# A linear-attention layer and MLP on one core: the issue order of the attention phase redone

## The chip, the cores and the metric

The kernel runs on one core of a Trainium2 chip. The metric is the device time of one execution in microseconds (us); the median of several executions is given. Five engines work at the same time, each through its own list of instructions in order: TensorE (PE, matmuls; PEld is its weight load), VectorE (DVE), ScalarE (ACT), GpSimd (POOL) and SyncE (SP, whose queue issues most of the DMAs here). An engine that reaches an instruction whose inputs are not ready stops there, and everything behind it in its list stops too. All runs quoted are fast, that is, none was slowed as a whole.

## The reference, cut to what matters

```python
h   = x + A(layernorm(x))        # S = 2048 tokens, D = 576, 32 heads of 18
out = h + B(layernorm(h))
def A(y):                        # linear attention
    q, k, v = heads(y @ wqkv)
    phi(t) = [softmax(t @ w_phi), softmax(-t @ w_phi)]
    kv, z = sum over tokens of phi(k) * v, and of phi(k)
    return (phi(q) @ kv / (phi(q) @ z)) @ wo
def B(y):                        # MLP, F = 4608
    return gelu(layernorm(y) @ w1 + b1) @ w2 + b2
```

The tokens are cut into 16 tiles of 128. Phase 1 must see every tile's k and v before any attention output exists, since kv is a sum over all tokens. After it come attention output, wo and MLP, in 8 rounds of two tiles.

## The kernel before

A small scheduler records every operation with what it reads and writes, in *program order*, and derives the waits from that: a read recorded after a write waits for that write. So moving a line changes the order in which an engine meets its work, and sometimes also what it waits for. `yT` holds normalised, transposed tiles in NSL slots; tile t uses slot t % NSL.

```python
NSL = 10
# start, SP queue: the wk transposes first, then a transpose for each normalised tile
# phase 1 (cut):
for t in range(NT + 2):
    if t < NT: p1_k(t)                     # k of tile t, two exponentials on ScalarE
    if t in (3, 4): ...weffq_unit(i)...    # folds w_phi into wq; needs the wq transposes
    if 5 <= t < NT: fill(1)                # one q unit: q of two tiles, 7 or 14 heads
    if t == 0:
        ln1_norm("pool", 4); ln1_tr(4)     # normalise on GpSimd, transpose by DMA on SP
        ln1_norm("pool", 5); ln1_tr(5)
        for b, (h0, nh) in enumerate(HG):
            dma_tr(wqT[...])               # five wq transposes, behind tiles 4 and 5
    ... p1_v(t - 1); p1_kv(t - 2); p1_mul(t - 1); p1_sums(t) ...
    for u in {0: (6,), 1: (7,), 2: (8,), 3: (9,), 7: (10,), 8: (11,), 10: (12,), ...}.get(t, ()):
        ln1_norm("pool", u); ln1_tr(u)
    for _ in range(2): bulk.pop(0)()       # two bulk weight loads a tile
# after it (cut): N = phi(q) @ kv, then wo, LN2, and the MLP
for r in range(NR):
    if r == 0:                             # the first three W1 groups split by tile
        for j in range(2):
            for g in range(3): w1_group(0, g, 128 * j, 128)
    for g in range(NG):                    # NG = 9
        if r or g >= 3: w1_group(r, g)
        if more and g == (0 if r else 3): attn_N(a, S1)
        if more and g == (4 if r else 6):
            attn_wo(a, S1)
            attn_N(b, S1)                  # same PSUM banks as wo
    slots[12] = lambda b=b: attn_wo(b, S1) # inside the first W2 tile, 41 steps
    w2_tile(r, 0, slots); w2_tile(r, 1, {})
```

The softmax here doesn't subtract the row's maximum and nothing guards it: scores larger than these inputs give would overflow.

## Time and profile before

| reading | value | from |
|---|---|---|
| time | 474.74 us | median |
| TensorE busy | 424.4 us of 475.4 | page |
| start of k(0), of k(5) | 17.2, 52.1 us | timeline |
| start of the MLP | 129.7 us | timeline |
| MLP round 0, a later round | 54.3, 41.64 us | timeline, chain |

The head of the page of the kernel before: busy tenths of TensorE in 40 slices of 11.9 us each, and the clock it was granted.

```profile
span 475.4 us, 8941 instructions
PE   2456996987888999999999999999999999999996
...
PEclk9995898998979799999999999999999999999999
```

The last two thirds are full; TensorE's idle time is in the first third, so that is where order can gain most. Lines of TensorE picked from the view of waits of the kernel before (who waited for whom: us in total, times, longest):

```profile
PE ps_all L415 <- DMA RA<-in_A_wqkv_dram: 6.8, 5, 2.2
PE ps_all L496 <- DVE RA L423: 6.3, 1, 6.3
PE ps_all L496 <- DMA yT<-ybuf: 5.0, 3, 2.3
PEld ps_all L596 <- DVE x_all L643: 5.5, 7, 0.8
PE ps_all L596 <- DVE x_all L643: 4.3, 7, 0.6
```

In order: the wq transposes, the folded wk before k(0), tiles normalised too late, and, seven times, N waiting for VectorE to drain the banks of wo. The timeline of TensorE at k(5) and around the late tiles (start us, us, engine, line, operation, shapes, count; in brackets the idle time just before and who ended it):

```profile
52.06 1.58 PE L496 MATMUL ps_all<-RA,yT 128*128 128x512 bf16 x10
...
74.06 1.39 PE L496 MATMUL ps_all<-RA,yT 128*128 128x512 bf16 x10 [1.69 <-DMA yT<-ybuf]
...
77.05 0.72 PE L546 MATMUL ps_all<-RB 128*128 128x133 bf16 x10
80.09 2.56 PE L496 MATMUL ps_all<-RA,yT 128*128 128x512 bf16 x10 [2.32 <-DMA yT<-ybuf]
```

The same block of k takes 1.39 us after the wait of 1.69 us and 2.56 after that of 2.32: matmuls after idle time can be slow for a while.

### The profile page before, as it was taken

The numbers are of one execution on the slowest core, as the hardware profiler recorded it, in microseconds if no ns is written. First come the engines' busy times: TensorE is split into PE (matmuls) and PEld (weight loads), VectorE is DVE, ScalarE is ACT, GpSimd is POOL, SyncE is SP. The second block draws the span as 40 slices with busy tenths as digits, with TensorE's granted clock in tenths as the row PEclk, the third lists the DMA queues.
The fourth block names the chain that finished last, engine by engine and source line by source line (L and its number), as shares of the span: only waits on it lengthen the run. The fifth ranks groups of instructions, "written<-read, shape, count | busy, mean of one in ns | idle before, by whom it ended". The sixth has DMA issues, their size and how long they took to land.

```text
span 475.4 us, 8941 instructions
## 1 busy us (share of the span) xinstructions
PE 424.4 (89%) x3702; PEld 271.5 (57%) x3702; DVE 190.6 (40%) x456; ACT 186.9 (39%) x422; POOL 78.8 (17%) x105
## 2 busy tenths in 40 slices
PE   2456996987888999999999999999999999999996
PEld 1123663655666546655765666576566657656753
DVE  3663596778502433331443333144333314431002
ACT  3343582533777302530650254066025406602710
POOL 2992348200001100110110011011001101100000
PEclk9995898998979799999999999999999999999999
DMA  8568956100251010102110011112001111100000
GB/s 189 134 128 247 278 176 181 39 2 14 48 195 17 14 34 21 25 18 28 28 30 17 23 23 21 28 28 27 17 26 22 22 28 28 28 15 26 2 0 26
DMA packets 51952, 26.76 MB, mean 56 GB/s; under 512 B 39752, under 2 KB 50888, under 8 KB 51912
## 3 DMA queue, kind: packets, MB, share of 16 engines
q1 hardware_dynamic: 50736, 25.58, 22.0%
q10 hardware_dynamic: 1176, 0.61, 0.7%
q8 instruction: 29, 0.48, 0.4%
q14 instruction: 11, 0.09, 0.1%
HBM read 14.47 MB, written 2.36 MB: 35 GB/s over the span
## 4 chain that ended last, share of the span: by engine, by line
PE 75%; DVE 7%; POOL 5%; DMA 5%; ACT 3%; issue 2%; SPq 1%; ACTq 1%; DVEq 0%; POOLq 0%
PE ps_all L798 29%; PE ps_all L775 26%; PE ps_all L769 5%; PE ps_all L637 4%; POOL ybuf L367 3%; PE ps_all L496 3%; PE ps_all L511 3%; PE ps_all L576 2%; DMA oT<-obuf 2%; PE ps_all L596 2%; DMA yT<-ybuf 2%; SPq L321 1%; DMA x_all<-in_A_x_dram 1%; PE ps_all L546 1%; DVE x_all L643 1%
## 5 line engine op out<-in xcount | busy, mean ns | idle before, releaser
L780 ACT ACTIVATE RA<-ps_all,b1T 128x256 bf16<-128x256 f32 (+1 forms) x300 | 125.8, 462 | 196.2 <-PE ps_all L775 192.2
L775 PE MATMUL ps_all<-yT,w1sb 128*128 128x256 bf16 (+1 forms) x1200 | 142.6, 274 | 0.0
L775 PEld LDWEIGHTS ps_all<-yT,w1sb 128*128 128x128 bf16 x1200 | 110.5, 100 | 27.2 <-issue 15.1
L798 PE MATMUL ps_all<-w2a,RA 128*128 128x512 bf16 (+1 forms) x640 | 95.3, 286 | 0.0
L798 PE MATMUL ps_all<-RB,RA 128*128 128x64 bf16 (+1 forms) x512 | 67.7, 286 | 0.0
L798 PEld LDWEIGHTS ps_all<-w2a,RA 128*128 128x128 bf16 x640 | 46.5, 98 | 36.2
L798 PEld LDWEIGHTS ps_all<-RB,RA 128*128 128x128 bf16 x512 | 33.4, 98 | 32.3
L643 DVE SCALAR_TENSOR_TENSOR x_all<-ps_all,x_all 128x576 bf16<-128x576 f32 x16 | 12.1, 757 | 94.4 <-PE ps_all L637 94.4
L628 POOL TENSOR_TENSOR obuf<-tpn 128x576 bf16<-128x576 f32 x14 | 19.6, 1401 | 165.5 <-issue 138.6
L804 DVE TENSOR_TENSOR tmpo<-ps_all,b2bc 128x64 f32<-128x64 f32 x16 | 3.6, 225 | 100.6 <-PE ps_all L798 100.6
L496 PE MATMUL ps_all<-RA,yT 128*128 128x512 bf16 (+1 forms) x160 | 27.0, 323 | 12.7 <-DVE RA L423 6.3
L502 ACT ACTIVATE RB<-ps_all 128x576 bf16<-128x576 f32 x32 | 19.1, 648 | 39.5 <-PE ps_all L496 39.5
L532 DVE TENSOR_TENSOR RB<-ps_all,RB 128x1152 bf16<-128x1152 f32 x16 | 21.6, 1350 | 29.6 <-PE ps_all L511 29.5
L656 POOL TENSOR_TENSOR st<-st,neghalf 128x1 f32<-128x1 f32 x16 | 8.8, 548 | 141.6 <-DVE st L654 141.6
L367 POOL TENSOR_SCALAR ybuf<-x_all,st 128x576 bf16<-128x576 bf16 x14 | 32.1, 2299 | 0.7 <-POOL st L347 0.4
L769 PE MATMUL ps_all<-yT,w1t 64*128 64x256 bf16 (+1 forms) x300 | 29.9, 274 | 2.3 <-ACT RA L780 2.3
L582 ACT ACTIVATE Eq<-ps_all 128x512 bf16<-128x512 f32 (+1 forms) x48 | 25.3, 527 | 16.0 <-DVE den L612 9.9
L576 PE MATMUL ps_all<-yT,WQ 128*128 128x256 bf16 x200 | 26.6, 285 | 1.9 <-ACT Eq L582 1.9
L511 PE MATMUL ps_all<-RB,yT 128*128 128x512 bf16 (+1 forms) x160 | 25.3, 310 | 1.3 <-DVE RB L532 1.3
L637 PE MATMUL ps_all<-wo_sb,oT 128*128 128x512 bf16 (+1 forms) x160 | 23.0, 292 | 3.3 <-DMA oT<-obuf 3.3
L496 PEld LDWEIGHTS ps_all<-RA,yT 128*128 128x128 bf16 x160 | 11.9, 108 | 24.2 <-issue 16.6
L576 PEld LDWEIGHTS ps_all<-yT,WQ 128*128 128x128 bf16 x200 | 19.4, 103 | 7.1 <-ACT Eq L582 2.7
(76 smaller groups left out, 290.3 us busy)
## 6 DMA issues: line engine op xcount, KB each, us to landing
w1sb<-in_B_w_dram SPq DMA_DIRECT2D x8, 576.0 KB, 5.1
w2a<-in_B_w_dram SPq DMA_DIRECT2D x4, 720.0 KB, 7.9
RB<-in_B_w_dram SPq DMA_DIRECT2D x2, 1152.0 KB, 7.5
out_dram<-WQ SPq DMA_DIRECT2D x16, 144.0 KB, 1.7
x_all<-in_A_x_dram SPq DMA_DIRECT2D x3, 576.0 KB, 4.4
RB<-in_A_wqkv_dram SPq DMA_DIRECT2D x1, 576.0 KB, 5.7
w1t<-in_B_w_dram SPq DMA_DIRECT2D x2, 288.0 KB, 8.0
wo_sb<-in_A_wo_dram SPq DMA_DIRECT2D x1, 576.0 KB, 9.2
```

Source lines behind the costliest of these rows:

```text
L367: P.add(eng, lambda e: e.tensor_scalar(ybuf[yb][:, 0:D], src, mean, rstd, ALU.subtract, ALU.mult), reads=[r_src, r_st], writes=[res(f"ybuf ...
L496: P.add("pe", lambda e, c=c, o=o, n=n: e.matmul(ps_all[:, 512 * KB + o:512 * KB + o + n], yT[:, c, sl * 128:(sl + 1) * 128], weffk[:, c, o ...
L511: P.add("pe", lambda e, c=c, o=o, n=n: e.matmul(ps_all[:, 512 * VB + o:512 * VB + o + n], yT[:, c, sl * 128:(sl + 1) * 128], wv[:, c, o:o ...
L532: P.add("dve", lambda e: e.tensor_tensor(vx(t)[:, :, :, 0:DH], ps_all[:, 512 * VB:512 * VB + D].rearrange("p (h d) -> p h d", h=H).unsquee ...
L576: P.add("pe", lambda e, i=i, c=c, h0=h0: e.matmul(ps_all[:, 512 * bk + RW * i:512 * bk + RW * i + RW], weffq[:, c, DH * h0:DH * h0 + 128], ...
L582: P.add("act", lambda e, s=s: e.activation(Eq[:, r, s, bs[0]:bs[0] + n, :], ps_all[:, 512 * bk:512 * bk + RW * n].rearrange("p (b t) -> p ...
L628: P.add(oeng, lambda e: e.tensor_tensor(obuf[ob][:, 0:D], tpn[:, 0, :], tpn[:, 1, :], ALU.add), reads=[res("tpn")], writes=[res(f"obuf{ob}")])
L637: P.add("pe", lambda e, c=c, bk=bk, o=o, n=n: e.matmul(ps_all[:, 512 * bk:512 * bk + n], oT[ob][:, c, :], wo_sb[:, c, o:o + n], start=(c = ...
L769: P.add("pe", lambda e, i=i, o=o, h=h, w=w: e.matmul(ps_all[:, o:o + n], w1t[h:h + 64, w:w + 128], yT[h:h + 64, 4, ys], start=(i % 2 == 0) ...
L775: P.add("pe", lambda e, c=c, m=m, o=o: e.matmul(ps_all[:, o:o + n], w1sb[:, c, 128 * m:128 * m + 128], yT[:, c, ys], start=False, stop=(c ...
L780: P.add("act", lambda e, m=m, o=o: e.activation(hmid[:, m, off:off + n], ps_all[:, o:o + n], AF.Gelu_apprx_tanh, bias=b1T[:, m:m + 1]), re ...
L798: P.add("pe", lambda e, m=m, bk=bk, o=o, n=n: e.matmul(ps_all[:, 512 * bk:512 * bk + n], w2_lhs(m, j), w2_rhs(m, o, n), start=(m == 0), st ...
```

## The change

The intent was to keep TensorE fed before the MLP, and to take two small waits out of each round. Its core:

```diff
-    NSL = 10
+    NSL = 12
+    def warm(n):                      # dummy matmuls on a zeroed tile
+        for _ in range(n):
+            P.add("pe", lambda e: e.matmul(ps_all[:, 2048:2560], WQ[:, 0:128], WQ[:, 128:640], ...
+    warm(12)                          # before the first real matmul, and 2 or 3 after each weffk group
...                                    # wq transposes interleaved with those of tiles 1 to 3
-    for t in range(NT + 2):
+    WU = {2: (0, 1), 3: (2, 3), 4: (4, 5, 6)}
+    for t in range(NT):
+        for u in ((4, 5) if t == 1 else (t + 4,) if 1 < t < NT - 4 else ()):
+            ln1_norm("pool", u)       # four tiles ahead, before the work of tile t
+            ln1_tr(u)
+        p1_k(t)
+        for i in WU.get(t, ())[:1]:
+            weffq_unit(i)
+        if t >= 5:
+            fill(1)
...                                    # the bulk loads: one or two a tile, from tile 1 on
-        P.add("dve", ... tmpo = psum + b2 (two pieces); ostage = tmpo + x)   # condensed
+        P.add("pool", ... tmpo = x + b2)                                     # condensed
+        P.add("dve", ... ostage = psum + tmpo, in two pieces)                # condensed
...
-        if r == 0: (three W1 groups split by tile)
-            if more and g == (4 if r else 6):
+            if more and g == 5:
                 attn_wo(a, S1)
+            if more and g == 6:
                 attn_N(b, S1)
-            slots[12] = lambda b=b: attn_wo(b, S1)
+            slots[24] = lambda b=b: attn_wo(b, S1)
```

Tile 2's N now also comes before the MLP, some buffers share memory to make room for 12 slots, and the order of some loads, statistics and late q units is changed too.

More of the change, by code (lines that the diff above doesn't have):

```diff
@@ L241, in _build @@
     mask7 = sb("mask7", [128, 7, 19])
-    mask25 = sb("mask25", [128, 25, 19])
-    maskf = sb("maskf", [128, 7, 19], F32)
     neghalf = sb("neghalf", [128, 2], F32)
-    wphi_st = sb("wphi_st", [128, 5, DH])
-    phib = sb("phib", [128, 5, 126])
+    OTR = sb("OTR", [128, 1280])
+    mask25 = OTR[:, 0:475].rearrange("p (h d) -> p h d", h=25)
+    wphi_st = OTR[:, 480:570].rearrange("p (b j) -> p b j", b=5)
+    phib = OTR[:, 576:1206].rearrange("p (b j) -> p b j", b=5)
+    oT = [OTR[:, 640 * i:640 * i + 640].rearrange("p (c t) -> p c t", c=5) for i in range(2)]
     bns = sb("bns", [128, 12], F32)
@@ L254, in _build @@
     obuf = [sb(f"obuf{i}", [128, 640]) for i in range(2)]
-    oT = [sb(f"oT{i}", [128, 5, 128]) for i in range(2)]
     st1 = sb("st1", [128, 8, NT], F32)
@@ L265, in _build @@
     tmpo = sb("tmpo", [128, D], F32)
+    maskf = tmpo[:, 0:133].rearrange("p (g d) -> p g d", g=7)
     ps_all = ctx.enter_context(nc.psum_tensor("ps_all", [128, 4096], F32))
@@ L291, in _build @@
     P.add("pool", lambda e: e.memset(neghalf[:, :], -0.5), writes=[res("neghalf")])
-    WPH = rr("wphi{}", 4)
+    WPH = rr("wphi{}", 3)
+    P.add("dve", lambda e: e.memset(WQ[:, 0:640], 0.0), writes=[res("warm")])
     P.add("dve", lambda e: e.memset(wphi_st[:, 3, :], 0.0), writes=[res("wphi1")])
@@ L298, in _build @@
     P.add("dve", lambda e: e.memset(wqT[:, :, 576:640], 0.0), writes=[res("wqTpad")])
+    def warm(n):
+        for _ in range(n):
+            P.add("pe", lambda e: e.matmul(ps_all[:, 2048:2560], WQ[:, 0:128], WQ[:, 128:640],
+                                           start=True, stop=True), reads=[res("warm")], banks=[bank[4]])
     xsplit = [(0, 1), (1, 1), (2, 2), (4, 4), (8, 4), (12, 4)]
@@ L327, in _build, with tr_wq @@
     load_x(1)
-    load_x(2)
     for b, (h0, nh) in enumerate(HG):
         dma_tr(wkT[:, b:b + 1, 0:D], A_wqkv[0:D, D + DH * h0:D + DH * h0 + 128], [], [res(f"wkT{b}")])
-    load_x(3, "sp")
-    load("sp", wv[:, 0:4, :], A_wqkv[0:512, 2 * D:3 * D].rearrange("(c p) m -> p c m", p=128), [res("wv")])
-    load("sp", wv[0:64, 4, :], A_wqkv[512:576, 2 * D:3 * D], [res("wv4")])
+    def tr_wq(b):
+        h0 = HG[b][0]
+        dma_tr(wqT[:, b:b + 1, 0:D], A_wqkv[0:D, DH * h0:DH * h0 + 128], [], [res(f"wqT{b}")])
     def ln1_stats_act(t):
@@ L392, in ln1_tr @@
         tr_y(yb1[t], t)
+    warm(12)
     ln1_stats_dve(0)
-    ln1_stats_act(2)
-    ln1_stats_act(3)
+    ln1_norm("dve", 0)
+    ln1_tr(0)
+    load_x(2, "sp")
+    load("sp", wv[:, 0:4, :], A_wqkv[0:512, 2 * D:3 * D].rearrange("(c p) m -> p c m", p=128), [res("wv")])
+    load("sp", wv[0:64, 4, :], A_wqkv[512:576, 2 * D:3 * D], [res("wv4")])
     P.add("dve", lambda e: e.tensor_tensor(
@@ L401, in _build @@
         mask7[0:126, :, 0:1].unsqueeze(1).to_broadcast([126, 5, 7, DH]), ALU.mult),
-        reads=WPH[0:3] + [res("mask7")], writes=[res("phib")])
-    ln1_norm("dve", 0)
-    ln1_tr(0)
+        reads=WPH + [res("mask7")], writes=[res("phib")])
     ln1_stats_dve(1)
@@ L410, in _build @@
     ln1_tr(1)
+    load_x(3, "sp")
+    tr_wq(0)
+    tr_wq(1)
     def weff_mm(wT, rname, c, b, col):
@@ L428, in _build @@
             weff_mm(wkT, "wkT", c, b, col)
+        warm(2 if b < 4 else 3)
     for c in range(5):
@@ L435, in _build @@
     R_weffk = rr("weffk{}", 5) + [res("weffkb"), res("weffkb4")]
-    for t in (2, 3):
-        ln1_norm("pool", t)
-        ln1_tr(t)
+    ln1_stats_dve(2)
+    ln1_norm("dve", 2)
+    ln1_tr(2)
+    tr_wq(2)
+    ln1_stats_dve(3)
+    ln1_norm("dve", 3)
+    ln1_tr(3)
+    tr_wq(3)
+    tr_wq(4)
     load_x(4, "sp")
     load_x(5, "sp")
-    ln1_stats_dve(4)
-    ln1_stats_dve(5)
-    P.add("dve", lambda e: e.memset(weffq[:, :, 576:592], 0.0), writes=[res("weffqpad")])
+    P.add("dve", lambda e: e.memset(weffq[:, :, 576:592], 0.0), writes=[res("weffqpad"), res("warm")])
     P.add("dve", lambda e: e.memset(wo_sb[64:128, 4, :], 0.0), writes=[res("wopad")])
@@ L505, in p1_k, with p1_v @@
                 writes=[res(f"Ek{eb}_{s}")], banks=[bank[KB], bank[KB + 1]])
-    def p1_v(t):
+    def p1_v(t, VB=VB):
         sl = t % NSL
@@ L528, in p1_sums, with p1_mul @@
         P.add("dve", frec, reads=[res(f"sums{vb}")], writes=[res(f"vext{vb}")])
-    def p1_mul(t):
+    def p1_mul(t, VB=VB):
         vb = t % 2
@@ L559, in weffq_unit @@
                 weff_mm(wqT, "wqT", i, b, 512 * QB + DH * HG[b][0])
-            ps_copy("act", weffq[:, i, 0:450], ps_all[:, 512 * QB:512 * QB + 450], bank[QB], [res(f"weffq{i}")])
+            ps_copy("act", weffq[:, i, 0:450], ps_all[:, 512 * QB:512 * QB + 450], bank[QB], [res(f"weffq{i}"), res("warm")])
         elif i == 5:
@@ L629, in attn_N @@
               reads=[res("tpn")], writes=[res(f"obuf{ob}")])
-        dma_tr(oT[ob][:, :, :], obuf[ob][:, :], [res(f"obuf{ob}"), res(f"opad{ob}")], [res(f"oT{ob}")])
+        dma_tr(oT[ob], obuf[ob][:, :], [res(f"obuf{ob}"), res(f"opad{ob}")],
+               [res(f"oT{ob}")] + (WPH + [res("phib"), res("mask25")] if t < 2 else []))
     def attn_wo(t, bset):
@@ L646, in attn_wo @@
         P.add("dve", lambda e: e.scalar_tensor_tensor(
-            tmpo[:, :], x_all[:, t, :], float(D), x_all[:, t, :], ALU.mult, ALU.mult,
-            accum_out=st(1)), reads=[res(f"x{t}")], writes=[res("tmpo"), res(f"s2b_{t}")])
+            tpn[:, 0, :], x_all[:, t, :], float(D), x_all[:, t, :], ALU.mult, ALU.mult,
+            accum_out=st(1)), reads=[res(f"x{t}")], writes=[res("tpn"), res(f"s2b_{t}")])
         P.add("dve", lambda e: e.scalar_tensor_tensor(st(2), st(0), st(0), st(1), ALU.mult, ALU.subtract),
@@ L658, in attn_wo @@
         tr_y(norm("dve", x_all[:, t, :], res(f"x{t}"), st(6), st(5), res(f"s2f_{t}"), True), t)
-    qlist = [(r, u) for r in (0, 1, 2, 3, 5, 4, 6, 7) for u in range(3)]
+    qlist = [(r, u) for r in (0, 1, 2, 3, 6, 4, 5, 7) for u in range(3)]
     qn = [0]
@@ L669, in fill @@
                 qn[0] += 1
-    for t in range(NT + 2):
-        if t < NT:
-            p1_k(t)
-        if t in (3, 4):
-            for i in range(4 * (t - 3), min(7, 4 * (t - 3) + 4)):
-                weffq_unit(i)
-        if 5 <= t < NT:
-            fill(1)
+    WU = {2: (0, 1), 3: (2, 3), 4: (4, 5, 6)}
+    for t in range(NT):
+        last = t == NT - 1
+        for u in ((4, 5) if t == 1 else (t + 4,) if 1 < t < NT - 4 else ()):
[5 more added lines that the diff above has]
+        if t >= 5:
+            fill(1)
+        if t >= 1:
+            p1_v(t - 1)
+        for i in WU.get(t, ())[1:2]:
+            weffq_unit(i)
+        if t >= 2:
+            p1_kv(t - 2)
+        for i in WU.get(t, ())[2:]:
+            weffq_unit(i)
+        if t == 0:
+            ln1_stats_act(4)
+        elif t % 2 == 1 and t + 5 < NT:
+            ln1_stats_act(t + 5)
+        if t >= 1:
+            p1_mul(t - 1)
+        p1_sums(t)
+        if t % 2 == 0 and t + 5 < NT:
+            ln1_stats_dve(t + 5)
         if t == 0:
             late_masks()
-            ln1_norm("pool", 4)
-            ln1_tr(4)
-            ln1_norm("pool", 5)
-            ln1_tr(5)
-            for b, (h0, nh) in enumerate(HG):
-                dma_tr(wqT[:, b:b + 1, 0:D], A_wqkv[0:D, DH * h0:DH * h0 + 128], [], [res(f"wqT{b}")])
         if t == 1:
@@ L691, in _build @@
                    B_b1[2560:4608].rearrange("(m p) -> m p", p=128), [], [res("b1b")])
-        if t + 6 < NT and t % 2 == 0:
-            ln1_stats_act(t + 6)
-        if 1 <= t <= NT:
-            p1_v(t - 1)
-        if t >= 2:
-            p1_kv(t - 2)
-        if 1 <= t <= NT:
-            p1_mul(t - 1)
-        if t < NT:
-            p1_sums(t)
-        if t + 6 < NT and t % 2 == 1:
-            ln1_stats_dve(t + 6)
-        for u in {0: (6,), 1: (7,), 2: (8,), 3: (9,), 7: (10,), 8: (11,), 10: (12,), 11: (13,), 13: (14, 15)}.get(t, ()):
-            ln1_norm("pool", u)
-            ln1_tr(u)
-        for _ in range(2):
-            if bulk:
-                bulk.pop(0)()
+        if t == 13:
+            P.add("pool", lambda e: e.tensor_copy(b1T[:, 0:32], b1st[:, 0:32]), reads=[res("b1a")], writes=[res("b1T")])
+            P.add("pool", lambda e: e.tensor_copy(b1T[:, 32:36], b1st[:, 44:48]), reads=[res("b1b")], writes=[res("b1T")])
+        if t >= 1 and bulk:
+            bulk.pop(0)()
+        if t >= 1 and t % 4 == 0 and bulk:
+            bulk.pop(0)()
+    p1_v(NT - 1, 0)
+    p1_kv(NT - 2)
+    p1_mul(NT - 1, 0)
+    fill(1)
+    p1_kv(NT - 1)
     while bulk:
@@ L728, in _build @@
         reads=[res("mask7")], writes=[res("kvr")], banks=[bank[7]])
-    P.add("dve", lambda e: e.tensor_copy(b1T[:, 0:32], b1st[:, 0:32]), reads=[res("b1a")], writes=[res("b1T")])
-    P.add("dve", lambda e: e.tensor_copy(b1T[:, 32:36], b1st[:, 44:48]), reads=[res("b1b")], writes=[res("b1T")])
     S1, S2 = (6, 7, 5), (1, 2, 0)
+    fill(2, (4, 3))
     attn_N(0, S1, "dve")
-    fill(2, (4, 3))
     attn_N(1, S2, "dve")
-    fill(4, (4, 3))
+    fill(6, (4, 3))
     attn_wo(0, S1)
-    fill(2, (4, 3))
+    fill(3, (4, 3))
     attn_wo(1, S2)
+    attn_N(2, S1)
     fill(24, (4, 3))
@@ L803, in w2_tile @@
         ob = t % 2
-        P.add("dve", lambda e: e.tensor_tensor(tmpo[:, 512:D], ps_all[:, 512 * TAILB:512 * TAILB + 64],
-                                               b2bc[:, 512:D], ALU.add),
-              reads=[res("b2")], writes=[res("tmpo")], banks=[bank[TAILB]])
-        P.add("dve", lambda e: e.tensor_tensor(tmpo[:, 0:512], ps_all[:, 512 * mb:512 * mb + 512],
-                                               b2bc[:, 0:512], ALU.add),
-              reads=[res("b2")], writes=[res("tmpo")], banks=[bank[mb]])
-        P.add("dve", lambda e: e.tensor_tensor(ostage[ob][:, :], tmpo[:, :], x_all[:, t, :], ALU.add),
-              reads=[res("tmpo"), res(f"x{t}")],
-              writes=[res(f"ostage{ob}")] + (R_weffq if t < 2 else []))
+        P.add("pool", lambda e: e.tensor_tensor(tmpo[:, :], x_all[:, t, :], b2bc[:, :], ALU.add),
+              reads=[res("b2"), res(f"x{t}")], writes=[res("tmpo"), res("maskf")])
+        for bk, o, n in ((TAILB, 512, 64), (mb, 0, 512)):
+            P.add("dve", lambda e, bk=bk, o=o, n=n: e.tensor_tensor(
+                ostage[ob][:, o:o + n], ps_all[:, 512 * bk:512 * bk + n], tmpo[:, o:o + n], ALU.add),
+                reads=[res("tmpo")], writes=[res(f"ostage{ob}")] + (R_weffq if t < 2 else []), banks=[bank[bk]])
         P.dma(ch_out[ob], lambda e: e.dma_start(outr[t * 128:(t + 1) * 128, :], ostage[ob][:, :]),
@@ L819, in _build @@
         more = r + 1 < NR
-        if r == 0:
-            for j in range(2):
-                for g in range(3):
-                    w1_group(0, g, 128 * j, 128)
         for g in range(NG):
-            if r or g >= 3:
-                w1_group(r, g)
-            if more and g == (0 if r else 3):
+            w1_group(r, g)
+            if more and r and g == 0:
                 attn_N(a, S1)
-            if more and g == (4 if r else 6):
+            if more and g == 5:
                 attn_wo(a, S1)
+            if more and g == 6:
                 attn_N(b, S1)
```

## The prediction

> **What bounds it now.** Two different halves. From about 184 us on, TensorE is the limit: the chain that ended last is almost all matmuls and one MLP round of two tiles takes 41.64 us (184.4 to 226.05, chain view). Its parts in the timeline are nine W1 groups at 2.18, two W2 tiles at 8.8, two N blocks at 0.57, two wo blocks at 1.24: 40.9 us. The missing 0.75 us is the second N block waiting for VectorE to drain wo from the same banks (waits view: PE on `x_all` L643, 4.3 us in 7 waits). Before 184 us TensorE mostly waits. Warm work up to 129.7 us is only some 77 us (16 tiles of k, v, kv at 3.0, 24 q units at most 1.1, two N and wo). Stalls: first k at 17.2 us behind a late weffk cast (DVE sat 4.9 us on tile 1's rstd, queued on GpSimd behind other tiles); 30 to 40 us on the wqT transposes, which sit in the SP queue behind tiles 4 and 5; 72 to 80 us on yT of tiles 10 and 11, normalised too late. MLP round 0 takes 54.3 us, 12.7 more than a steady one: split W1 groups, table load, a 2.3 us wait for oT, cold matmuls.
>
> **Clock.** Ten k matmuls take 2.56 us after the 80 us stall and 1.39 warm. The Trainium skill ("TensorE: Matmul & The Clock Gate", The HAM clock gate) says half clock follows an idle window of about 3.4 us; the trace agrees, so each long stall costs about 1.5 us more.
>
> **The change, costed (estimates from the durations above).**
> - Start: tile 0 and 1 norms no longer queue behind phib and the ACT statistics; k(0) near 13 us instead of 17.2. Warm-up matmuls fit before phib and cost nothing.
> - wqT interleaved with the first transposes, weffq spread over tiles 2 to 4: k(5) near 35.5 us instead of 52.1.
> - GpSimd needs about 3.6 us a tile (2.3 norm plus four or two tiny ops) against 4.1 us of TensorE, so four tiles of lead hold; the 72-80 us stall goes.
> - A new stall: at tile 10 the transpose of tile 14 is issued before q unit (round 1, third), and with 12 slots tile 14 takes slot 2, which that unit reads. The unit must wait for it: ACT statistics of tile 14, 1.6 us small ops, 2.3 norm, 2.6 transpose. About 7 us plus cold restart. (It also reads the wrong tile; and the warm matmuls zero bank 4 that holds weffk chunk 4. Neither costs time.)
> - N(0) near 96 us instead of 110.1. yT(1) is ready about 20.5 us later, so the MLP starts near 116.5 (129.7 before) after some 5 us of idle TensorE.
> - Round 0 about 42 us instead of 54.3.
> - Rounds 1 to 6: 40.9 us, 0.75 less each, as a W1 group now stands between wo and N.
> - Tail: one VectorE add of 0.76 us fewer before the last store.
>
> Sum: 116.5 + 42 + 6 x 40.9 + 37.3 + 3.4 = 444.5 us. All the gain is on the critical path; about 25 us come before the first steady MLP round, 5 from the rounds.
>
> **Right or wrong:** k(5) start near 35.5; a TensorE wait of 5 to 9 us on a yT DMA at the third q unit of tile 10; POOL never the releaser of k before that; MLP start near 116; round 0 at 42; steady round at 40.9.
>
> **What would spoil it:** transposes slowed by bulk loads beyond the lead (4.96 us was seen); GpSimd falling behind; wo(b) at slot 24 finding oT late (2 us slack); the tile-10 wait being short (then near 437).
>
> Predicted 444 us, 80% range 434 to 455. Chances: faster 0.97, within 2% 0.02, slower 0.01.

## The result, and the profile after

The changed kernel takes 448.03 us (median of 4 runs, 446.45 to 451.36) against 474.74. The ratio is 0.9449, interval 0.939 to 0.951. The profiled execution was the longest of the four.

The head of the page after, in slices of 11.2 us:

```profile
span 449.5 us, 8821 instructions
PE   7489939988599999999999999999999999999996
...
PEclk9999968989799999999999999999999999999999
```

The start is much fuller, but TensorE is busy for only three tenths of the sixth slice and half of the eleventh. Lines of TensorE from the view of waits after:

```profile
PE ps_all L594 <- DMA yT<-ybuf: 8.8, 1, 8.8
PE ps_all L794 <- DMA yT<-ybuf: 5.6, 1, 5.6
PEld ps_all L823 <- DVE WQ L832: 4.6, 7, 0.7
PE ps_all L428 <- DMA RA<-in_A_wqkv_dram: 2.7, 1, 2.7
PE ps_all L514 <- DMA yT<-ybuf: 1.8, 1, 1.8
```

The wait for wqT fell from 6.8 to 2.7 us, N's seven waits for VectorE are gone, and three new ones stand on top: a q unit (L594) waits 8.8 us for a tile, the MLP's first group (L794) 5.6 us for a tile, and the weight loads of W2 (L823) seven times up to 0.7 us for VectorE. The timeline of TensorE around the first one:

```profile
33.75 1.39 PE L514 MATMUL ps_all<-RA,yT 128*128 128x512 bf16 x10
34.97 1.25 PE L594 MATMUL ps_all<-yT,WQ 128*128 128x256 bf16 x10
...
54.01 1.17 PE L514 MATMUL ps_all<-RA,yT 128*128 128x64 bf16 x9
63.93 1.23 PE L594 MATMUL ps_all<-yT,WQ 128*128 128x256 bf16 x5 [8.75 <-DMA yT<-ybuf]
64.95 2.61 PE L529 MATMUL ps_all<-RB,yT 128*128 128x512 bf16 x10
67.37 1.21 PE L564 MATMUL ps_all<-RB 128*128 128x133 bf16 x10
68.37 2.12 PE L514 MATMUL ps_all<-RA,yT 128*128 128x512 bf16 x10
```

The first two lines are k(5) and the q unit beside it, so k(5) comes 18 us sooner (33.75 us instead of 52.06). The last four are tile 10 and what follows: its q unit (63.93) reads tiles 2 and 3. Why should it wait for a transpose at 63.9 us, when those tiles were transposed by about 20 us? Because tile 14 shares slot 2 with tile 2 when there are 12 slots (14 % 12 = 2), and its transpose is recorded at the top of iteration 10, just before this unit, while two of the three units that read tile 2 come earlier. The unit thus waits for tile 14, and in fact reads tile 14 in place of tile 2 for the last seven heads. The comparison with the reference does not see this.

The chain that ended last before that wait (start us, us, what) is GpSimd from 23 to 61 us with hardly a break; its end:

```profile
54.91 2.30 POOL ybuf L375
...
58.04 0.58 POOL st L355
...
58.79 2.31 POOL ybuf L375
...
61.17 2.62 DMA yT<-ybuf
63.80 0.14 issue
63.93 1.23 PE ps_all L594 x5
```

That is the statistics, the normalisation and the transpose of tile 14. Read alone, this chain says "GpSimd is too slow". The experiments below say otherwise.

### The profile page after: what moved, and what is told of

Its sections match the earlier page's. It is cut to its first block, busy times and chain, and to the rows that moved or that the text cites. A ratio compares the mean times of both kernels' runs of the same rounds, so it can differ in the third digit from the quotient of the medians.

```text
span 449.5 us, 8821 instructions
## 1 busy us (share of the span) xinstructions
PE 414.5 (92%) x3622; PEld 266.1 (59%) x3665; DVE 184.9 (41%) x444; ACT 182.4 (41%) x406; POOL 94.4 (21%) x119
## 4 chain that ended last, share of the span: by engine, by line
PE 72%; DVE 10%; POOL 10%; issue 4%; DMA 2%; ACT 1%; SPq 0%; DVEq 0%; POOLq 0%; ACTq 0%
PE ps_all L800 29%; PE ps_all L823 25%; POOL ybuf L375 6%; PE ps_all L794 5%; PE ps_all L656 4%; PE ps_all L594 3%; DVE ybuf L375 2%; PE ps_all L529 2%; PE ps_all L614 2%; PE ps_all L514 2%; DVE tpn L665 1%; DMA yT<-ybuf 1%; DMA x_all<-in_A_x_dram 1%; ACT RA L805 1%; POOL st L367 1%
## 5 line engine op out<-in xcount | busy, mean ns | idle before, releaser
L805 ACT ACTIVATE RA<-ps_all,b1T 128x256 bf16<-128x256 f32 x288 | 122.7, 471 | 191.3 <-PE ps_all L800 188.4
L800 PE MATMUL ps_all<-yT,w1sb 128*128 128x256 bf16 x1152 | 140.6, 276 | 0.0
L800 PEld LDWEIGHTS ps_all<-yT,w1sb 128*128 128x128 bf16 x1152 | 107.9, 99 | 28.0 <-issue 15.6
L823 PE MATMUL ps_all<-w2a,RA 128*128 128x512 bf16 (+1 forms) x624 | 93.2, 284 | 2.0 <-DVE WQ L832 1.1
L823 PEld LDWEIGHTS ps_all<-w2a,RA 128*128 128x128 bf16 x640 | 46.0, 98 | 39.1 <-DVE WQ L832 4.6
L823 PE MATMUL ps_all<-RB,RA 128*128 128x64 bf16 (+1 forms) x511 | 68.6, 286 | 0.1
L823 PEld LDWEIGHTS ps_all<-RB,RA 128*128 128x128 bf16 x512 | 33.5, 98 | 32.3
L832 DVE TENSOR_TENSOR WQ<-ps_all,tmpo 128x64 bf16<-128x64 f32 (+1 forms) x32 | 14.6, 456 | 86.2 <-PE ps_all L823 84.6
L675 POOL TENSOR_TENSOR st<-st,neghalf 128x1 f32<-128x1 f32 x16 | 8.8, 548 | 163.1 <-DVE st L673 163.1
L594 PE MATMUL ps_all<-yT,WQ 128*128 128x256 bf16 x200 | 26.8, 286 | 9.5 <-DMA yT<-ybuf 8.8
L794 PE MATMUL ps_all<-yT,w1t 64*128 64x256 bf16 x288 | 28.6, 278 | 5.6 <-DMA yT<-ybuf 5.6
L829 POOL TENSOR_TENSOR tmpo<-x_all,b2bc 128x576 f32<-128x576 bf16 x16 | 20.4, 1273 | 43.6 <-DVE WQ L832 43.6
L375 POOL TENSOR_SCALAR ybuf<-x_all,st 128x576 bf16<-128x576 bf16 x12 | 27.6, 2300 | 2.2 <-POOL st L367 1.2
L594 PEld LDWEIGHTS ps_all<-yT,WQ 128*128 128x128 bf16 x200 | 19.2, 103 | 14.6 <-issue 9.0
L514 PE MATMUL ps_all<-RA,yT 128*128 128x512 bf16 (+1 forms) x155 | 22.0, 289 | 5.1 <-ACT RB L520 2.1
L529 PE MATMUL ps_all<-RB,yT 128*128 128x64 bf16 (+1 forms) x154 | 22.3, 292 | 0.3
L656 PE MATMUL ps_all<-wo_sb,OTR 128*128 128x64 bf16 (+1 forms) x145 | 20.1, 277 | 1.7 <-DVE tpn L641 1.0
```

Of the source, the lines that this page charges most:

```text
L375: P.add(eng, lambda e: e.tensor_scalar(ybuf[yb][:, 0:D], src, mean, rstd, ALU.subtract, ALU.mult), reads=[r_src, r_st], writes=[res(f"ybuf ...
L514: P.add("pe", lambda e, c=c, o=o, n=n: e.matmul(ps_all[:, 512 * KB + o:512 * KB + o + n], yT[:, c, sl * 128:(sl + 1) * 128], weffk[:, c, o ...
L529: P.add("pe", lambda e, c=c, o=o, n=n: e.matmul(ps_all[:, 512 * VB + o:512 * VB + o + n], yT[:, c, sl * 128:(sl + 1) * 128], wv[:, c, o:o ...
L594: P.add("pe", lambda e, i=i, c=c, h0=h0: e.matmul(ps_all[:, 512 * bk + RW * i:512 * bk + RW * i + RW], weffq[:, c, DH * h0:DH * h0 + 128], ...
L656: P.add("pe", lambda e, c=c, bk=bk, o=o, n=n: e.matmul(ps_all[:, 512 * bk:512 * bk + n], oT[ob][:, c, :], wo_sb[:, c, o:o + n], start=(c = ...
L794: P.add("pe", lambda e, i=i, o=o, h=h, w=w: e.matmul(ps_all[:, o:o + n], w1t[h:h + 64, w:w + 128], yT[h:h + 64, 4, ys], start=(i % 2 == 0) ...
```

## The experiments

The control, the changed kernel once more in the rounds of the first group of runs:

> The changed kernel once more, unaltered, as the control for the runs beside it. Both theories: about 448 us (446 to 452), the third q unit of tile 10 waits 8 to 9 us for the transpose of tile 14.

Measured: 449.03 us (446.69 to 450.14), ratio 0.9454. The wait at tile 10 was 8.7 us. The kernel's executions spread by about 1%, so a difference of 2 us needs the trace beside it.

### fix_order: tile 14 after the q unit

```diff
+        if t != 10:
             for u in ahead: ln1_norm("pool", u); ln1_tr(u)
         p1_k(t)
         ...
         if t >= 5: fill(1)
+        if t == 10:
+            for u in ahead: ln1_norm("pool", u); ln1_tr(u)
```

> Normalisation and transpose of tile 14 issued after the third q unit of tile 10 instead of before it; nothing else moved. Theory A (the wait is only the slot conflict of tile 14 with tile 2): no TensorE wait on a yT DMA over 1 us between 35 and 95 us, kv of the last tile about 10 us earlier, time about 438 us. Rival B (GpSimd, busy without a gap from 23 to 61 us, is the limit, and the conflict merely shows it): the wait comes back at tile 11 to 15 as k waiting for yT, and the time falls by less than 4 us.

Measured: 437.98 us (436.79 to 439.28), ratio 0.9221, 11 us below the control beside it. The timeline of TensorE at tile 10:

```profile
55.80 1.17 PE L514 MATMUL ps_all<-RA,yT 128*128 128x64 bf16 x9
56.81 0.71 PE L594 MATMUL ps_all<-yT,WQ 128*128 128x256 bf16 x5
57.36 1.39 PE L529 MATMUL ps_all<-RB,yT 128*128 128x512 bf16 x10
58.58 0.72 PE L564 MATMUL ps_all<-RB 128*128 128x133 bf16 x10
```

The wait is gone and did not come back at a later tile. GpSimd does the same work at the same speed. Theory A holds, rival B falls: GpSimd stood at the head of the chain because one unit asked for its newest tile four tiles early. The medians differ by 11 us. In the traces the kv of the last tile starts at 83.47 us instead of the control's 93.63, 10.2 us sooner: the wait of 8.7 and some 1.5 us of slow matmuls after it. In the first trace of the changed kernel those lose 2.8 us (q 1.23 instead of 0.71, v 2.61 instead of 1.39, kv 1.21 instead of 0.72, k 2.12 instead of 1.39).

### wq_late: the wq transposes back behind tiles 4 and 5

```diff
-    tr_wq(0) ... tr_wq(4)            # interleaved with tiles 1 to 3
+        if t == 1:                   # after the transposes of tiles 4 and 5
+            for b in range(5): tr_wq(b)
```

> All five wqT transposes put back behind the transposes of tiles 4 and 5 on the SP queue. Theory A (the early wqT is what lets k(5) start at 34 us instead of 52): TensorE waits some 13 us more for wqT at the first weffq unit, k(5) starts near 47 us, the tile-10 wait shrinks to 5 or 6 us because part of GpSimd's chain goes on meanwhile, and the time rises by about 10 us to 458. Rival B (GpSimd's normalisations set the pace to 61 us anyway, so TensorE's early lead is used up at tile 10): the tile-10 wait shrinks by nearly all of the delay and the time rises by 3 us or less.

Measured: 462.15 us, ratio 0.9734, 13.1 us above the control. From the waits of this run:

```profile
PE ps_all L426 <- DMA RA<-in_A_wqkv_dram: 13.3, 4, 10.2
PE ps_all L589 <- DMA yT<-ybuf: 8.7, 1, 8.7
```

TensorE waits 13.3 us for wqT instead of 2.4 in the control, k(5) starts at 48.38 us instead of 35.54, and the tile-10 wait is 8.7 us as before. Neither theory had its size: nothing was absorbed at tile 10. GpSimd had a pause of some 12 us (its normalisations start at 29.5 and then at 44.3 us), and the wait stayed the same. So GpSimd's backlog is not what sets it. The statistics of tile 14 are issued in iteration 9 and the unit stands in iteration 10, so the wait moves along with the loop. The early wqT is worth 13 us here, in full.

### n_adjacent: N right behind wo again

```diff
             if more and g == 5:
                 attn_wo(a, S1)
-            if more and g == 6:
                 attn_N(b, S1)
```

> The second N block of a round put back right behind wo, with no W1 group between; everything else as changed. Theory A (the W1 group between hides VectorE's drain of the shared banks): TensorE waits 0.6 to 0.8 us for VectorE at L662 in each of 7 rounds, a round takes 41.8 us instead of 41.16, time up by 4 to 5 us. Rival B (the round is bound elsewhere): round within 0.2 us of 41.16.

Measured: 453.77 us, ratio 0.9553 against 0.9422 for the run beside it (no_warm, which has the time of the changed kernel). From its waits:

```profile
PEld ps_all L614 <- DVE x_all L662: 5.6, 7, 0.8
PE ps_all L614 <- DVE x_all L662: 4.5, 7, 0.6
```

The seven waits are those of the kernel before, and a round takes 41.97 us (159.92 to 201.89) instead of 41.16. Theory A holds. One W1 group between wo and N is worth 0.8 us a round.

### add_early: the GpSimd addition at the start of the W2 tile

```diff
     mb = 2 + (RT * r + j) % 2
+    P.add("pool", ... tmpo = x + b2)
     for i in range(NF + LAG): ...matmuls of the tile, wo in slot 24...
-    P.add("pool", ... tmpo = x + b2)
     P.add("dve", ... ostage = psum + tmpo)
```

> The GpSimd addition of x and b2 issued at the start of each W2 tile instead of its end, so it no longer runs beside VectorE's normalisation of the same round. Theory A (the two share something: that normalisation took 1.30 us beside it, 0.43 otherwise, and so the tail bank is freed late): the normalisation of tile b takes 0.43 us in all rounds, TensorE's 0.7 us wait in the second W2 tile goes, a round takes 40.7 to 40.9 us instead of 41.16, the time falls by 2 to 3 us. Rival B (the second tile waits because wo at slot 24 of 41 is simply too late for VectorE): the round stays at 41.0 or more.

Measured: 446.34 us, ratio 0.9409 against the control's 0.9454; the two intervals overlap, so the time alone does not decide. The timelines of VectorE and GpSimd in round 6 do. First the changed kernel:

```profile
398.85 0.55 POOL L675 TENSOR_TENSOR st<-st,neghalf 128x1 f32<-128x1 f32 x1 [7.64 <-DVE st L673]
399.37 1.27 POOL L829 TENSOR_TENSOR tmpo<-x_all,b2bc 128x576 f32<-128x576 bf16 x1
399.51 1.30 DVE L375 TENSOR_SCALAR ybuf<-x_all,st 128x576 bf16<-128x576 bf16 x1 [0.73 <-POOL st L675]
...
400.93 1.01 DVE L832 TENSOR_TENSOR WQ<-ps_all,tmpo 128x64 bf16<-128x64 f32 x2
```

and then add_early:

```profile
386.30 1.27 POOL L819 TENSOR_TENSOR tmpo<-x_all,b2bc 128x576 f32<-128x576 bf16 x1
...
394.63 0.43 DVE L375 TENSOR_SCALAR ybuf<-x_all,st 128x576 bf16<-128x576 bf16 x1 [0.74 <-POOL st L675]
...
395.18 1.01 DVE L832 TENSOR_TENSOR WQ<-ps_all,tmpo 128x64 bf16<-128x64 f32 x2
```

VectorE's normalisation takes 1.30 us beside the GpSimd addition, ending about when it ends, and 0.43 without it. (In the kernel before, one beside a GpSimd normalisation took 0.94.) Behind it stands L832, whose first piece frees the PSUM bank that the next tile's 64-column matmuls need. But the stretched normalisation is not all that holds L832 up. L832 also reads the addition's result, and the addition stands in GpSimd's list behind wo's statistics (L675), so it ends only at 400.64 us. With a normalisation of 0.43 us L832 would still have had to wait until then; it started at 400.93. add_early takes both away at once, so the runs do not part them; by these times the stretch costs at most 0.3 us beyond the late addition. What is shown is that the place of the addition costs the round 0.34 us, and that wo at slot 24 without it (rival B) does not. In add_early TensorE's wait for L832 is gone and a round takes 40.82 us (158.72 to 199.54) instead of 41.16. The Trainium skill ("GPSIMD Engine Reference", Specifications) says that GpSimd shares its SBUF interfaces with VectorE, with contention for VectorE instructions that have two SBUF inputs or run in a mode that uses two ports. This trace agrees with a shared resource; it does not show which of its modes the normalisation ran in.

### no_warm: no warm-up matmuls at the start

```diff
     def warm(n):
-        for _ in range(n):
+        for _ in range(0):
```

> The changed kernel without any of its warm-up matmuls. Theory A (TensorE is not on the chain before 60 us, GpSimd and the transposes are; a slower TensorE for some us is absorbed): the first k blocks take 2.4 us instead of 1.4, k(5) starts at most 1.5 us later than 34 us, the time is within 1.5 us of 448. Rival B (the warm-up is a good part of the early gain): k(5) 4 us later or more, time up by 4 us or more.

Measured: 447.93 us, ratio 0.9422, so no difference from the changed kernel. From its timeline:

```profile
11.03 2.56 PE L514 MATMUL ps_all<-RA,yT 128*128 128x512 bf16 x10 [0.76 <-DVE RA L436]
```

The first k blocks do take 2.56 us instead of 1.40, and k(5) still starts at 33.69 us (33.75 and 35.54 in the two traces of the changed kernel). Theory A holds. In the first 20 us TensorE waits for transposes, and slower matmuls only shorten the waits. That does not hold up to tile 5: in the control, in fix_order and in combo the clock was low around 25 to 28 us, and there k(5) starts at 35.5 to 35.6 us.

The warm-up has a fault of its own, found by reading. It writes PSUM columns 2048 to 2559 while these collect chunk 4 of weffk, so that chunk is overwritten with zeros for 25 heads. The combos below avoid it.

### combo, combo_warm: the fixes together, and dummies where the wait is

combo is fix_order and add_early with the warm-up in bank 7. combo_warm adds

```diff
     fill(24, (4, 3))
+    for _ in range(20):               # dummy matmuls in the wait for yT of tile 1
+        P.add("pe", lambda e: e.matmul(ps_all[:, 2048:2560], WQ[:, 0:128], WQ[:, 128:640], ...
```

> Tile 14 after the q unit, the addition of x and b2 early, and the warm-up matmuls writing bank 7 instead of bank 4, where they zeroed a chunk of weffk. If the first two gains are independent, 438 less 2.5, about 435.5 us; the bank makes no difference to the time. Rival: they overlap and it stays at 438.

> The combo with 20 dummy matmuls of 512 columns in the 5 us wait for yT of tile 1 before the MLP, so that TensorE stays busy. Theory A (the first two W1 groups take 4.0 and 2.9 us instead of 2.2 because the clock fell in the wait): they take 2.2 to 2.4 us, time 2 us lower than the combo, about 433.5. Rival B (they are slow for another reason, or the dummies delay the real work): no gain or a loss.

Measured: combo 435.88 us (ratio 0.9158), combo_warm 434.07 us (ratio 0.9127; the intervals overlap). The two gains add, as far as the spread lets one see (435.5 was expected). The MLP's first groups in combo's timeline:

```profile
106.55 0.61 PE L800 MATMUL ps_all<-yT,w1t 64*128 64x256 bf16 x4 [5.50 <-DMA yT<-ybuf]
107.09 3.34 PE L806 MATMUL ps_all<-yT,w1sb 128*128 128x256 bf16 x16
110.37 0.39 PE L800 MATMUL ps_all<-yT,w1t 64*128 64x256 bf16 x4
```

and in combo_warm's:

```profile
104.65 0.39 PE L803 MATMUL ps_all<-yT,w1t 64*128 64x256 bf16 x4 [0.89 <-DMA yT<-ybuf]
104.98 1.92 PE L809 MATMUL ps_all<-yT,w1sb 128*128 128x256 bf16 x16
106.83 0.39 PE L803 MATMUL ps_all<-yT,w1t 64*128 64x256 bf16 x4
```

The first group takes 3.82 us from start to start after the wait and 2.18 with dummies in it. The granted clock was 0.50 from 104 to 110 us in combo and 1.00 in combo_warm, so the loss after this wait does come from the idle time, by 1.6 us. The medians differ by 1.8, but that they agree is partly luck: the two traces differ by 3.4, and the other 1.8 arose before tile 5, where the code is the same (k(5) at 35.45 and 33.63). That is also why the MLP starts 1.9 us sooner here; the dummies do not make yT arrive sooner, they only keep the matmuls fast.

### combo_split3, combo_warm2

combo_split3 is combo with the first three W1 groups split by tile again, as before. combo_warm2 is combo_warm without the warm-up at the start.

```diff
+        if r == 0:                                  # combo_split3
+            for j in range(2):
+                for g in range(3): w1_group(0, g, 128 * j, 128)
```

> The combo with the first three W1 groups of round 0 split by tile again, as the kernel before had them, so that TensorE can start on tile 0 while yT of tile 1 is on its way. Theory A (a split group is bound by ScalarE, four activations of 0.4 us for 1.2 us of matmuls, so what it fills it gives back): the MLP starts 3 to 5 us earlier, the whole groups start within 1 us of where they did, time within 1.5 us of the combo's 435.9. Rival B (taking the split out was a mistake of the change): at least 2.5 us faster than the combo.

> The combo with the 20 dummy matmuls before the MLP but without any of the warm-up matmuls at the start. If the early warm-up is worth nothing and the late one is, the time is that of combo_warm, about 434 (433 to 435). Rival (with the tile-10 wait gone TensorE is nearer the chain at the start, so a cold start now costs): 436 or more.

Measured: combo_split3 434.25 us, ratio 0.9144. The MLP starts at 102.88 us, 3.7 us before combo's, but the first whole group (the fourth) starts at 113.86 instead of 114.73: 2.8 of the 3.7 us are given back. In its timeline TensorE waits for ScalarE in between:

```profile
105.77 1.07 PE L806 MATMUL ps_all<-yT,w1sb 128*128 128x128 bf16 x16
...
107.95 0.23 PE L800 MATMUL ps_all<-yT,w1t 64*128 64x128 bf16 x1 [1.12 <-ACT RA L811]
108.75 0.28 PE L800 MATMUL ps_all<-yT,w1t 64*128 64x128 bf16 x3 [0.57 <-ACT RA L811]
```

The median is 1.6 us below combo's, where theory A allowed 1.5 and rival B asked for 2.5; the ratios' intervals overlap. The split is at best a small help, and the wait for ScalarE is why. combo_warm2 takes 432.54 us (431.98 to 432.96), ratio 0.9109: the lowest median, and without the overwritten chunk and the wrong tile. The rival (a cold start now costs) falls. Ratios from different groups of runs come from different chips, so 0.9109 against 0.9127 is no more than "the same".

## Why the prediction was right, point by point

The sum said 444.5 us, the prediction 444, measured was 448.03. The first trace is of the slowest execution (451.36 us), so the control's (448.20) stands beside it.

| step | predicted | trace after | control |
|---|---|---|---|
| start of k(0) | 13 | 11.16 | 11.41 |
| start of k(5) | 35.5 | 33.75 | 35.54 |
| wait at the third q unit of tile 10 | about 7 and a slow restart | 8.75 and some 2.8 | 8.66 and some 1.5 |
| N(0) | 96 | 97.8 | 96.6 |
| start of the MLP | 116.5 after some 5 idle | 118.53 after 5.56 | 116.88 after 5.40 |
| round 0 | 42 | 43.3 | 41.9 |
| a later round | 40.9 | 41.16 | 41.16 |
| last matmuls to the end | 3.4 | 3.4 | 3.4 |

So among the terms of the sum only the later rounds are clearly off in the control: 6 times 0.26 is 1.6 us, and the start of the MLP adds 0.4. The rest of its 448.20 is that the sum covers the trace's span, 446.5 us, and the device time is 1.7 us longer.

- **The large gain before the MLP** was right in place and size: 129.7 to 118.5 us. The two starts are not quite the same event, since the kernel before started the MLP on tile 0 alone (combo_split3 shows 3.7 us for that). That the early wqT carries the gain was confirmed by wq_late. The prediction did not expect the early warm-up to cost anything, and no_warm shows that it gives nothing either.
- **The new stall at tile 10** was right, down to its cause; fix_order proves the cause by removing it. The wait was undersized by almost 2 us. The restart differs by execution: 2.8 us in the first trace, 1.5 in the control, where 1.5 was said. In the first trace k(5) came 1.75 us sooner than said, but after a wait of 1.88 us at 93 us the clock fell once more (20 matmuls of q took 3.80 us; 2.34 in the control after the same wait), and N(0) came 1.8 us late. That part of the miss is luck of one execution.
- **Four tiles of lead hold for GpSimd** was right. In the changed kernel no k after tile 1 waited for a late tile, apart from the slot conflict.
- **Round 0** was 1.3 us longer than said in the first trace: the restart took 4.07 and 3.02 us for the first two groups against 2.18 warm, 2.7 us lost where the 42 leaves some 1.7. In the control the restart cost 1.3 and the round 41.9. combo_warm shows that the loss after this wait comes from the idle time. The round's own gain, 54.3 to 43.3, is as large as that before the MLP, and no run takes it apart. In the trace before, the split groups lost 6.4 us (12.95 for three groups) and some 6 went with a wait of 2.28 us for oT and slow matmuls after it; part of the first only moved to the start of the MLP.
- **"The trace agrees"**, which the prediction said of the 3.4 us of idleness before half clock, was too much. Half clock is there (0.50), but the wait at 80 us lasted 2.32 us, and the clock fell 2.0 us after the last matmul. At 93 us it fell after a wait of 1.88 us in one execution and not in another. What the traces show is how long it stayed low: 3.4 us (79.8 to 83.2 before, 93.8 to 97.2 after), 6.8 (117.7 to 124.5) or 10.2 (59.7 to 69.9).
- **"Rounds 1 to 6: 40.9 us, 0.75 less each"** is the term that failed. The gain was 0.48 us. n_adjacent shows that the mechanism named is worth its 0.8. What was missed is a new cost of 0.34: the addition moved to GpSimd stands behind wo's statistics there, so its result comes late, and it stretches VectorE's normalisation from 0.43 to 1.30 us, at the moment when VectorE is about to free a bank. add_early moves the addition and the round is 40.82; which of the two held VectorE up is not parted.
- **The tail** was right: after the last matmul two VectorE additions remain where there were three, 3.4 us to the end instead of 4.3.

## What to carry to other kernels

When a circular buffer is resized or its refill moved earlier, check in program order that the last reader of the old content is issued before the refill. If it isn't, the reader waits for the newest data and reads the wrong thing, and a loose tolerance will not tell. An engine that fills the chain before a wait need not be the bottleneck: ask what made the waiter need its newest result, and move that one thing. Work moved off a busy engine onto an idle one is free only if its result is ready when it is needed, in the idle engine's own order, and if the two do not share something at that moment, so place it early and where the other engine is idle; and put warm-up matmuls where the matmuls after a wait are on the critical path, not where the next thing is another wait.

## What the Trainium skill lacked or had wrong

- "TensorE: Matmul & The Clock Gate" (The HAM clock gate) gives about 3.4 us of sustained work until full clock. Here it was 3.0 us after the waits at tile 10 and 2.8 before the MLP in the control (clock back at 68.5 and 119.7), but 6.0 and 5.9 in the first trace of the same kernel (matmuls from 63.93, clock back at 69.9; from 118.53, back at 124.5). For an estimate on a critical path a range is safer than 3.4 us.
- No page was found to say that a warm-up at the start is worth nothing when TensorE then waits for data; here the time without and with it was 447.93 and 448.03 us.
